# Two early units' products on GpSimd, and token, weight and key steps at later places, in a fused attention and SwiGLU kernel

## The chip, the cores and the metric

The kernel runs on one core of one Trainium2 chip. The metric is the device time of one execution in microseconds (us); the figure for a kernel is the median of its runs. The engines are named as in the profile: PE is TensorE, DVE is VectorE, ACT is ScalarE, POOL is GpSimd, SP is the queue that issues most DMAs.

## The reference

Inputs are q, k, v of 4 batches, 4 heads, 1088 positions and 32 values each, two sketches S1 and S2 of 8 x 32, and the weights of a feed-forward block with 128 inputs and 1536 hidden columns.

```python
def phi(x):
    a = einsum('rd,bhsd->bhsr', S1, x)
    b = einsum('rd,bhsd->bhsr', S2, x)
    return einsum('bhsi,bhsj->bhsij', a, b).reshape(*x.shape[:-1], 64)
q_p, k_p = phi(q), phi(k)
kv  = einsum('bhsf,bhsd->bhfd', k_p, v)
z   = sum(k_p, axis=2)
num = einsum('bhsf,bhfd->bhsd', q_p, kv)
den = einsum('bhsf,bhf->bhs', q_p, z)[..., None] + 1e-06
x   = (num / den), heads side by side: 4352 tokens x 128
g   = x @ w_gate;  silu = g / (1 + exp(-g));  val = x @ w_val
out = (silu * val) @ w_out
```

## The kernel before

**Blocks and units.** The 4352 tokens are cut into ten blocks. Blocks 0, 1, 2 are batch 0 (384, 320 and 384 tokens); blocks 3 to 9 are the other batches in pieces of 480 (the last 384). The 1536 hidden columns are cut into 12 chunks of 128. A *unit* (i, j) is block i times chunk j: two products on TensorE (gate and value), SiLU of the gate on ScalarE, and the product of both, kept as `hidden[i, j]`. A *down* step (L1068) multiplies it with chunk j of w_out and sums it over j in PSUM.

**Plain units.** `unit` (L1008 to L1033) does a unit with fp32 matmuls: L1016 for gate and value, L1020 the SiLU into `sg`, and L1031 on VectorE, `sg` times the value in PSUM, into `hbuf` (or `late`, further rooms of the same kind). With `late=True` VectorE is left out: the SiLU goes to a slot of `room`, ScalarE copies the value out of PSUM (L1028), and the pair is put on the list `lates`. `catch_up` (L1037 to L1040) takes the oldest pair from that list and multiplies it on GpSimd. Four units are late before the change: (0,0), (0,1), (0,2), (1,0).

**Split units.** From (2,6) on, units use cut operands. `start_unit` (L974) multiplies the differences xd and wd for gate and value (L980) and scales the sums in place on ScalarE (L983). `finish_unit` (L985) adds the products of the upper and lower parts (L992, L993), then SiLU (L995) and the product on VectorE (L1000). Start comes one or two units ahead of finish. Three pairs of PSUM banks go round, so a start needs the pair that an L1000 has read.

**Cutting.** `cut_weights` (L839) cuts a group c of three chunks of w_gate or w_val in four steps, one at each call: w1 on ScalarE (L843), low = w - w1 (L846), wb on ScalarE (L848), wd (L851 on VectorE or L855 on GpSimd). Names like `v0`, `g1` in the code are the steps of w_val group 0 and w_gate group 1. Groups 2 and 3 belong to chunks 6 to 11, which block 2 uses first; groups 0 and 1 to chunks 0 to 5, which block 3 uses first. Groups g0, g1 and all v are cut on GpSimd. `cut_tokens` (L857) cuts a block's tokens in two steps: for block 2 (`x`) and block 3 it is L865 on ScalarE and L873 (xd) on VectorE in the first, L868 (x0) on VectorE in the second.

**Attention of the later batches.** `attentions` (L615) is a generator; `parts_of(1)` runs its next part, and `group()` the parts that hold TensorE work. For batch 1, 2 and 3: transposes of keys (`turn_keys`, L327) and queries (L578), products of keys with the sketches (L354), key features (L377), their sums on GpSimd (L547), sums with the values (L388, L713), `fold` on VectorE (L601, L605, L608, which writes a third sketch), `spread_out` (L723), products of the queries with the three sketches (L342), `query_step` (L741 to L758, ending in phT), and `numerators` (L776 on TensorE, L793 copies into the tokens xT).

**Order.** Everything is issued by hand, in program order on each engine. Which step stands where is set by tables: `steps_at` names cutting steps by the place in the loop after which they are issued (the three loops at L1305, L1327 and L1341, and the `while todo` loop at L1350, where the key is the number of down steps left), calls of `catch_up`, and the calls of `parts_of`. An engine takes its instructions in that order; an instruction that waits keeps all behind it on its engine.

**Batch 0, third step.** Around 20 to 30 us the features of block 2's queries (L461 copies on ScalarE, L475 on VectorE), their totals (L497 on TensorE) and the division (L518 to L539) are issued among the units (1,1), (1,2) and (0,3). Weights arrive as 64-bit words and are made fp32 in steps (L263 to L286), of which L286 for chunks 3 to 5 of w_val runs on GpSimd.

Of the kernel before, what the change touches and what calls it, by code (L numbers as in the profile page):

```python
# [19 lines left out]
def kernel(  # L20
# [91 lines left out]
    def bank(tag=None):  # L112

        if tag is not None:
            i = place[tag]
        else:
            i = place[free_banks[turn[0] % len(free_banks)]]
            turn[0] += 1
        touch(i)
        return PS[:, i, :]  # L120

    def pair(keep=None):

        i = min((i for i in (0, 4, 6) if i not in held), key=lambda i: max(used[i], used[i + 1]))
        touch(i, i + 1)
        if keep is not None:
            held.add(i)
            kept[keep] = i
        return PS[:, i : i + 2, :]
# [183 lines left out]
    late = const.tile([P, NL, BW], FP32, tag="late", name="late", bufs=1)  # L313
# [153 lines left out]
    def query_features(n, pss, qbs=None, phq=None, pairs=(0, 1)):  # L467
        w = 32 * n
        if phq is None:
            phq = apool.tile([P, H, 32 * XS], FP32, tag="phq", name="phq", bufs=2)  # L470
        qbs = qbs or [query_copy(n, *ps) for ps in pss]
        for pr in pairs:
            (both, parts), qb = pss[pr], qbs[pr]
            if both is not None:
                nc.vector.tensor_tensor(  # L475
                    out=phq[:, 2 * pr : 2 * pr + 2, 0:w],
                    in0=both[:, :, 0, 0:w], in1=qb[:, :, 0:w], op=ALU.mult,
                )
            else:
                for g in range(2):  # L480
                    nc.vector.tensor_tensor(
                        out=phq[:, 2 * pr + g, 0:w],
                        in0=parts[g][:, 0, 0:w], in1=qb[:, g, 0:w], op=ALU.mult,
                    )
        return phq

    def halves(x):
        return x if isinstance(x, list) else [x[:, 0, :], x[:, 1, :]]

    def totals(n, phq, kvz, nd, which=(1, 0)):  # L490

        w = 32 * n
        for t in which:
            for h in range(H):
                for half in range(2):
                    r = slice(F * half, F * half + F)
                    nc.tensor.matmul(  # L497
                        halves(nd[t])[half][32 * h : 32 * h + 32, 0:w],
                        kvz[t][r, 32 * h : 32 * h + 32],
                        phq[r, h, 0:w],  # L500
                        start=True,
                        stop=True,
                    )
        return nd

    def side_by_side(tag):
        both = wide(tag)[:].rearrange("p g (t w) -> p g t w", t=2)
        return both[:, :, 0, :], both[:, :, 1, :]
# [291 lines left out]
    todo = []  # L800
# [56 lines left out]
    def cut_tokens(i, engine=nc.gpsimd, soon=False):  # L857

        t0, n = blocks[i]
        x = xT[:, t0 : t0 + n]  # L860
        x1, x0, xd = x_parts[i] = [
            apool.tile([P, WB], F32R, tag=tag, name=name, bufs=2)
            for tag, name in (("qb", "x1"), ("dT", "x0"), ("rd", "xd"))
        ]
        nc.scalar.activation(x1[:, 0:n], x, AF.Copy, scale=CUT)  # L865

        def low():
            engine.tensor_tensor(  # L868
                out=x0[:, 0:n], in0=x, in1=whole(x1[:, 0:n]), op=ALU.subtract
            )  # L870

        def difference():
            nc.vector.scalar_tensor_tensor(  # L873
                out=xd[:, 0:n], in0=whole(x1[:, 0:n]), scalar=WHOLE, in1=x,
                op0=ALU.mult, op1=ALU.subtract,
            )


        first, second = (difference, low) if soon else (low, difference)
        first()  # L880
        yield
        second()
# [91 lines left out]
    def start_unit(i, j):  # L974

        n = blocks[i][1]
        xd = x_parts[i][2][:, 0:n]
        ps = sums_of[i, j] = pair((i, j))[:, :, 0:n]
        for k, w in enumerate((wg, wv)):
            nc.tensor.matmul(  # L980
                ps[:, k], w_parts[id(w), j // 3][2][:, j % 3, :], xd, start=True, stop=True
            )
        nc.scalar.activation(ps, ps, AF.Copy, scale=-1.0 / WHOLE)  # L983
# [24 lines left out]
    def unit(i, j, late=False, between=(None, None), apart=False):  # L1008


        t0, n = blocks[i]
        g, u = halves(pair()) if apart else (bank(), bank())
        for o, w in ((g, wg), (u, wv)):
            if between[0] and w is wv:
                between[0]()
            nc.tensor.matmul(  # L1016
                o[:, 0:n], w[:, j, :], xT[:, t0 : t0 + n], start=True, stop=True
            )
        sg = room[:, len(lates) + caught[0], :] if late else fpool.tile([P, WB], FP32, tag="sg", name="sg", bufs=5)
        nc.scalar.activation(sg[:, 0:n], g[:, 0:n], AF.Silu)  # L1020
        slot_of[i, j] = slots.pop(0)
        hj = slot_of[i, j]
        hidden[i, j] = hj
        todo.append((i, j))
        if late:
            if between[1]:
                between[1]()
            nc.scalar.copy(hj[:, 0:n], u[:, 0:n])  # L1028
            lates.append((hj[:, 0:n], sg[:, 0:n]))
        else:  # L1030
            nc.vector.tensor_tensor(  # L1031
                out=hj[:, 0:n], in0=sg[:, 0:n], in1=u[:, 0:n], op=ALU.mult
            )  # L1033
# [3 lines left out]
    def catch_up():  # L1037
        o, sg = lates.pop(0)
        caught[0] += 1
        nc.gpsimd.tensor_tensor(out=o, in0=o, in1=sg, op=ALU.mult)  # L1040
# [89 lines left out]
    def part(name, i):  # L1130

        next(fills[name, i], None)
# [47 lines left out]
    n = steps[0][1]  # L1180
# [50 lines left out]
    def parts_of(n):  # L1231

        for _ in range(n):
            if ahead[0] not in ("pe", "end"):
                ahead[0] = next(att, "end")
# [21 lines left out]
    qbs = [query_copy(steps[2][1], *ps) for ps in pss]  # L1257
    part("wv", 2)
    part("wg", 2)
    unit(1, 1)  # L1260
    phq = query_features(steps[2][1], pss, qbs)
    part("wv", 2)
    for _ in range(3):
        catch_up()
    unit(1, 2)
    nd = totals(steps[2][1], phq, kvz, side_by_side("a"))
    divide(0, *steps[2], nd)

# [25 lines left out]
    def at(*names):  # L1294
        for name in names:
            next(cuts[name], None)

    def next_down():
        if order:
            todo.remove(order[0])  # L1300
            todo.insert(0, order.pop(0))
        down()

    steps_at = {20: ("v2",), 21: ("v3", "v2", "v3"), 22: ("g2",), 23: ("g3",)}
    for z, (i, j) in enumerate(seq):  # L1305
# [15 lines left out]

    steps_at = {
        0: ("g2", "v2", "v3"), 1: ("g2",), 2: ("g2", "g3"), 3: ("g3", "v2"), 4: ("g3", "v3"), 5: ("g2",),
        6: ("x",), 7: ("x",), 8: ("g3", "v0"), 9: ("g0",), 10: ("v0",), 11: ("g0",),
    }
    ND = 13
    for n in range(ND):  # L1327
        if n == ND - 2:
            start_unit(2, 6)
        next_down()  # L1330
        parts_of(n in (0, 1, 7, 10, 11, 12))
        at(*steps_at.get(n, ()))
        if n == 5:
            catch_up()


    steps_at = {
        6: ("v0",), 7: ("g0",), 8: ("v1",), 9: ("g1",), 10: ("v0",), 11: ("g0", "v1"),
    }
    todo.sort(key=lambda x: (order + [x]).index(x))  # L1340
    for j in range(6, NCH):  # L1341
# [4 lines left out]
        parts_of(1)  # L1346
        at(*steps_at.get(j, ()))
    x_steps = iter(())
    steps_at = {9: ("g1",), 8: ("v1",), 6: ("g1",), 4: ("v1", "g1")}
    while todo:  # L1350
        if len(todo) == 2:
            start_unit(HEAD, 0)
        next_down()
        at(*steps_at.get(len(todo), ()))
        next(x_steps, None)
        if len(todo) == 7:
            parts_of(1)
            x_steps = cut_tokens(HEAD, nc.vector, soon=True)
            next(x_steps)
        if len(todo) < 5:  # L1360
            parts_of(1)

    flat = hbuf[:].rearrange("p s w -> p (s w)")
# [73 lines left out]
```

## Time and profile before

| what | before |
|---|---|
| median of 3 runs | 281.86 us (281.56 to 281.90) |
| profiled execution | 281.39 us, of which the span of the trace is 279.7 us |
| PE busy | 269.9 us, 97% of the span |
| DVE busy | 208.6 us, 75% |
| ACT busy | 188.9 us, 68% |
| POOL busy | 102.7 us, 37% |
| granted TensorE clock | 1.00 |
| DVE busy in 60 to 70 us, 90 to 100 us | 9.90 of 10, 9.38 of 10 |
| POOL busy in 60 to 70 us, 70 to 80 us, 90 to 100 us | 8.72, 6.97, 6.45 of 10 |

The span is the stretch between the first and the last instruction of the trace; the 1.69 us around it are counted in the device time. Busy times come from the profiled execution. A line of a timeline gives the start from the span's begin, the duration, engine, source line, operation, what is written and read, the shapes, how many instructions are merged, and in brackets the idle time just before with the engine and line that ended it. A duration includes time in which an instruction was held up after its start. An fp32 matmul of the program shows as two in the trace.

### The profile page before, as it was taken

To read this page: it belongs to the slowest core of one execution; us is meant where nothing else is said; L and a number is where in the kernel's file an instruction comes from. 1 tells how busy PE (TensorE), PEld (TensorE's weight loads), DVE (VectorE), ACT (ScalarE), POOL (GpSimd) and SP (SyncE) were. 2 spreads that over 40 slices of the span, in tenths; PEclk is the share of its full clock that TensorE was granted. 3 is DMA by queue.
4 is the path that set the end of the run, shared out by engine and by line. 5 is a ranking of instruction groups with operands and counts; after the bars stand their busy time and mean duration, and the time that the engine had idled before them with its cause. 6 is when DMAs were issued, how large, how long until landed. Compare 5 with 4: busy or idle time off the path is not lost.

```text
span 279.7 us, 5723 instructions
## 1 busy us (share of the span) xinstructions
PE 269.9 (97%) x2181; PEld 199.7 (71%) x2181; DVE 208.6 (75%) x355; ACT 188.9 (68%) x335; POOL 102.7 (37%) x112
## 2 busy tenths in 40 slices
PE   7898999999999889999999999999999999999995
PEld 7554466666785577777667768767887888788994
DVE  3996988879896962787736658867986995988431
ACT  3466566362693557676658898859879888886860
POOL 3312531249852650080014452534335462632000
PEclk9999999999999999999999999999999999999999
DMA  6572287131331042100200010000100200010011
GB/s 191 166 227 60 56 237 228 40 123 56 66 87 23 2 110 60 38 1 0 35 13 6 1 28 10 0 2 8 29 0 2 35 0 1 12 25 0 8 30 28
DMA packets 26139, 14.30 MB, mean 51 GB/s; under 512 B 19840, under 2 KB 24192, under 8 KB 26112
## 3 DMA queue, kind: packets, MB, share of 16 engines
q1 hardware_dynamic: 25456, 13.84, 19.3%
q8 instruction: 17, 0.28, 0.4%
q10 hardware_dynamic: 656, 0.10, 0.2%
q14 instruction: 10, 0.08, 0.1%
HBM read 11.41 MB, written 2.23 MB: 49 GB/s over the span
## 4 chain that ended last, share of the span: by engine, by line
PE 80%; DVE 12%; ACT 2%; issue 2%; DMA 1%; POOL 0%; SPq 0%; DVEq 0%; ACTq 0%
PE PS L1068 16%; PE PS L992 13%; PE PS L980 13%; PE PS L993 13%; PE PS L1016 10%; PE PS L1060 2%; PE PS L1063 2%; PE PS L1062 2%; PE PS L776 2%; PE PS L342 2%; DVE phk L377 2%; DMA kld<-in_k_dram 1%; PE PS L354 1%; PE PS L388 1%; DVE phT L758 1%
## 5 line engine op out<-in xcount | busy, mean ns | idle before, releaser
L983 ACT ACTIVATE PS<-PS 128x960 f32<-128x960 f32 (+1 forms) x90 | 83.3, 926 | 34.0 <-PE PS L980 33.1
L1000 DVE SCALAR_TENSOR_TENSOR hbuf<-PS,sg 128x480 f32<-128x480 f32 (+1 forms) x87 | 55.2, 634 | 42.9 <-ACT sg L995 40.3
L995 ACT ACTIVATE sg<-PS 128x480 f32<-128x480 f32 (+1 forms) x90 | 49.7, 552 | 2.6 <-ACT sg L995 1.3
L1068 PE MATMUL PS<-hbuf,wo 128*128 128x480 f32 (+3 forms) x118 | 45.8, 488 | 0.0
L980 PE MATMUL PS<-xd,graw 128*128 128x480 f32 (+1 forms) x69 | 38.2, 554 | 0.0
L980 PE MATMUL PS<-xd,wd 128*128 128x480 f32 (+1 forms) x90 | 33.5, 372 | 1.7 <-DVE hbuf L1000 1.7
L993 PE MATMUL PS<-x,wb 128*128 128x480 f32 (+1 forms) x90 | 33.4, 372 | 0.0
L992 PE MATMUL PS<-x,w 128*128 128x480 f32 (+1 forms) x90 | 33.4, 371 | 0.0
L1068 PEld LDWEIGHTS PS<-hbuf,wo 128*128 128x128 f32 x118 | 22.0, 189 | 5.6 <-issue 0.4
L980 PEld LDWEIGHTS PS<-xd,wd 128*128 128x128 f32 x90 | 17.0, 189 | 12.2 <-issue 5.8
L993 PE MATMUL PS<-x,graw 128*128 128x480 f32 (+1 forms) x69 | 25.5, 370 | 0.0
L1016 PE MATMUL PS<-xT,wv 128*128 128x384 f32 (+1 forms) x60 | 23.2, 468 | 0.6 <-POOL wv L286 0.3
L1016 PE MATMUL PS<-xT,wg 128*128 128x384 f32 (+1 forms) x60 | 23.5, 474 | 0.1
L1020 ACT ACTIVATE sg<-PS 128x384 f32<-128x384 f32 (+1 forms) x26 | 11.9, 466 | 15.7 <-PE PS L1016 14.8
L868 POOL TENSOR_TENSOR x<-xT,x 128x480 fp32r<-128x480 f32 (+1 forms) x6 | 7.2, 1192 | 39.5 <-ACT x L865 39.5
L980 PEld LDWEIGHTS PS<-xd,graw 128*128 128x128 f32 x69 | 13.0, 188 | 7.7 <-ACT PS L983 4.1
L992 PEld LDWEIGHTS PS<-x,w 128*128 128x128 f32 x90 | 16.9, 187 | 2.2
L993 PEld LDWEIGHTS PS<-x,wb 128*128 128x128 f32 x90 | 16.9, 188 | 2.1
L992 PE MATMUL PS<-x,graw 128*128 128x480 f32 (+1 forms) x48 | 18.4, 384 | 0.0
L1068 PE MATMUL PS<-hbuf,scaled 128*128 128x480 f32 x36 | 17.4, 564 | 0.0
L1016 PEld LDWEIGHTS PS<-xT,wv 128*128 128x128 f32 x60 | 11.1, 190 | 7.8 <-DVE hbuf L1031 1.0
L960 POOL TENSOR_TENSOR hlate<-hbuf,hlate 128x480 fp32r<-128x480 f32 x10 | 12.9, 1289 | 9.8 <-ACT hlate L959 7.7
(196 smaller groups left out, 541.1 us busy)
## 6 DMA issues: line engine op xcount, KB each, us to landing
kld<-in_k_dram SPq DMA_DIRECT2D x4, 544.0 KB, 4.0
vld<-in_v_dram SPq DMA_DIRECT2D x12, 144.0 KB, 4.0
qld<-in_q_dram SPq DMA_DIRECT2D x3, 544.0 KB, 3.4
raw<-in_moe_w_out_dram SPq DMA_DIRECT2D x4, 384.0 KB, 5.6
raw<-in_moe_w_gate_dram SPq DMA_DIRECT2D x3, 384.0 KB, 3.4
raw<-in_moe_w_val_dram SPq DMA_DIRECT2D x3, 384.0 KB, 3.1
out_dram<-o SPq DMA_DIRECT2D x16, 60.0 KB, 2.0
vld<-in_v_dram SPq DMA_DIRECT2D x4, 112.0 KB, 3.2
```

Source lines behind the costliest of these rows:

```text
L342: nc.tensor.matmul(ps[32 * a : 32 * a + 32, 96 * (c - c0) : 96 * (c - c0) + 96], qT[:, 4 * c + a, :], s123[:, a : a + H, :, :].rearrange(" ...
L868: engine.tensor_tensor(out=x0[:, 0:n], in0=x, in1=whole(x1[:, 0:n]), op=ALU.subtract)
L960: add_to(before, y + 2, lambda: nc.gpsimd.tensor_tensor(out=h0, in0=h, in1=whole(h1), op=ALU.subtract))
L980: nc.tensor.matmul(ps[:, k], w_parts[id(w), j // 3][2][:, j % 3, :], xd, start=True, stop=True)
L983: nc.scalar.activation(ps, ps, AF.Copy, scale=-1.0 / WHOLE)
L992: nc.tensor.matmul(ps[:, k], w1, x1, start=False, stop=False, skip_group_check=True)
L993: nc.tensor.matmul(ps[:, k], wb, x0, start=False, stop=True, skip_group_check=True)
L995: nc.scalar.activation(sg, ps[:, 0], AF.Silu, scale=WHOLE)
L1000: nc.vector.scalar_tensor_tensor(out=hj[:, 0:n], in0=ps[:, 1], scalar=WHOLE, in1=sg, op0=ALU.mult, op1=ALU.mult)
L1016: nc.tensor.matmul(o[:, 0:n], w[:, j, :], xT[:, t0 : t0 + n], start=True, stop=True)
L1020: nc.scalar.activation(sg[:, 0:n], g[:, 0:n], AF.Silu)
L1068: nc.tensor.matmul(acc[i][:, 0:n], w, hidden[i, j][:, 0:n], **sides)
```

## The change

Units (1,1) and (1,2) become late: L1031 on VectorE is replaced by the SiLU into `room`, the copy L1028 on ScalarE, and the product on GpSimd, and two more calls of `catch_up` are issued after the one that was there. The two steps of `x`, the token cut of block 2, are issued one place later, the first behind the part of `attentions` that holds the fold. The last two steps of `v0` and `g0`, and all steps of `v1` and `g1`, are issued later. In the last loop `parts_of` is called for 2, 3 and 4 remaining down steps and no longer for 1 and 0, so that the following parts (the keys' transposes of batch 3, then the queries' of batch 2) are issued from the next loop, which finishes a unit of block 3 before each.

```diff
-    unit(1, 1)
+    unit(1, 1, late=True)
     phq = query_features(steps[2][1], pss, qbs)
     part("wv", 2)
     for _ in range(3):
         catch_up()
-    unit(1, 2)
+    unit(1, 2, late=True)
...
     steps_at = {
         0: ("g2", "v2", "v3"), 1: ("g2",), 2: ("g2", "g3"), 3: ("g3", "v2"), 4: ("g3", "v3"), 5: ("g2",),
-        6: ("x",), 7: ("x",), 8: ("g3", "v0"), 9: ("g0",), 10: ("v0",), 11: ("g0",),
+        7: ("x",), 8: ("x", "g3", "v0"), 9: ("g0",), 10: ("v0",), 11: ("g0",),
     }
...
         at(*steps_at.get(n, ()))
-        if n == 5:
+        if n in (5, 6, 7):
             catch_up()
...
     steps_at = {
-        6: ("v0",), 7: ("g0",), 8: ("v1",), 9: ("g1",), 10: ("v0",), 11: ("g0", "v1"),
+        9: ("v0",), 10: ("g0", "v0"), 11: ("g0",),
     }
...
-    steps_at = {9: ("g1",), 8: ("v1",), 6: ("g1",), 4: ("v1", "g1")}
+    steps_at = {8: ("v1", "g1", "v1", "g1"), 6: ("v1", "g1"), 1: ("v1", "g1")}
...
-        if len(todo) < 5:
+        if len(todo) in (2, 3, 4):
             parts_of(1)
```

## Prediction

> **What bounds the kernel now.** I read the page first (busy times, then the chain that ended last), then what TensorE waited for, then the timelines of TensorE, VectorE, ScalarE and GpSimd around each of those waits. All times are us of the profiled execution: span 279.7, device time 281.39.
>
> ```profile
> PE 80%; DVE 12%; ACT 2%; issue 2%; DMA 1%; POOL 0%; SPq 0%; DVEq 0%; ACTq 0%
> ```
>
> ```profile
> PE PS L980 <- DVE hbuf L1000: 1.7, 1, 1.7
> PE PS L497 <- DVE phq L475: 1.0, 1, 1.0
> ...
> PE PS L342 <- DVE s L608: 0.3, 1, 0.3
> PE PS L1016 <- POOL wv L286: 0.3, 1, 0.3
> ...
> PE PS L776 <- DVE phT L758: 0.2, 1, 0.2
> ```
>
> TensorE has 97% busy and 80% of the chain. So only what shortens its few waits counts. The columns of the second view are waiter, releaser, us in total, times, longest. Listed are the five waits that the change can touch; they lie at 26.1 (L497), 28.5 (L1016), 72.7 (L342), 87.5 (L776) and 98.8 (L980). From 100 to 270 us it is busy 10.00 of every 10 us but once (9.92 from 180), so what is won before 100 is kept.
>
> Idle is measured to the modelled end of the last matmul, which lies later than the next one could start. I therefore count starts:
>
> ```profile
> 24.44 0.70 PE L1016 MATMUL PS<-xT,wv 128*128 128x320 f32 x2
> 26.11 1.23 PE L497 MATMUL PS<-phq,kvz 64*32 64x192 f32 x32 [0.96 <-DVE phq L475]
> 27.27 0.91 PE L1016 MATMUL PS<-xT,wg 128*128 128x384 f32 x2
> 28.49 0.91 PE L1016 MATMUL PS<-xT,wv 128*128 128x384 f32 x2 [0.31 <-POOL wv L286]
> ```
>
> Columns: start, duration, instruction. A 320-wide pair takes 0.54 from start to start elsewhere (23.90 to 24.44), a 384-wide one 0.645 (29.24 to 29.88). So L497 could start at about 25.08 (0.1 for the change of shape), 1.03 earlier, and the last line at 27.27 + 0.645, 0.57 earlier. The same count gives 0.5 at 72.7, 0.35 at 87.5, 1.85 at 98.8.
>
> Why is L475 late? VectorE and ScalarE there:
>
> ```profile
> 25.01 0.49 DVE L1031 TENSOR_TENSOR hbuf<-sg,PS 128x320 f32<-128x320 f32 x1 [2.30 <-ACT sg L1020]
> 25.41 1.01 DVE L475 TENSOR_TENSOR phq<-PS,qb 128x384 f32<-128x384 f32 x2
> ```
>
> VectorE stands still for 2.30 until the SiLU of unit (1,1) is there, at the head of its queue, while the data of L475 behind it (qb, L461, 22.85 to 23.72) is ready.
>
> The last wait, 98.8, is VectorE's queue again (first fence), with GpSimd beside it (second fence):
>
> ```profile
> 91.19 1.45 DVE L868 TENSOR_TENSOR x<-xT,x 128x480 fp32r<-128x480 f32 x1
> ...
> 94.64 1.77 DVE L377 TENSOR_TENSOR phk<-kab 128x512 f32<-128x512 f32 x1
> 96.34 0.83 DVE L327 STREAM_TRANSPOSE kT<-kld 128x640 f32<-128x640 f32 x1
> 97.10 0.53 DVE L1110 STREAM_TRANSPOSE o<-PS 128x384 f32<-128x384 f32 x1
> 97.56 0.66 DVE L327 STREAM_TRANSPOSE kT<-kld 128x512 f32<-128x512 f32 x1
> 98.16 0.61 DVE L1000 SCALAR_TENSOR_TENSOR hbuf<-PS,sg 128x480 f32<-128x480 f32 x1
> ```
>
> ```profile
> 91.08 1.05 POOL L855 TENSOR_TENSOR graw<-gphq,graw 128x384 fp32r<-128x384 f32 x1 [4.09 <-ACT graw L848]
> 94.28 1.58 POOL L547 TENSOR_TENSOR zs<-phk 128x512 f32<-128x512 f32 x1 [2.15 <-PE PS L1068]
> ```
>
> L1000 of (3,0), whose SiLU was done at 96.2, comes after two key transposes and an output transpose. And two VectorE operations are stretched exactly while GpSimd runs: L377 of 512 takes 0.67 alone and 1.77 beside L547.
>
> [...] (L868 1.45 beside L855; L377 1.77 beside L547; L377 with one input in PSUM 0.67 to 0.94 also beside GpSimd). The trace adds that they take turns: L547 asked at 94.28 and ran before the L377 that was queued for 94.64. [...] here 0.87 (L1040, 320 wide) against 0.47 (L1031). [...]
>
> **The change, part by part.** The order of instructions on TensorE and of the DMAs on SP is the same in both kernels, so only waits can change.
>
> (1) Units (1,1), (1,2) late. Off VectorE: two L1031, before L475 and before L518. Onto ScalarE: two L1028 of 0.44, behind the SiLUs: 24.64 + 4 steps of about 0.35 = 26.05. TensorE wants the banks that they free from 26.3 on; nothing else waits there (next ScalarE work is a SiLU at 27). Then VectorE: L475 at 23.35 and 23.85, done 24.3; L271 and L277 (their ScalarE inputs are done at 24.2 and 24.6), done 25.3; L286 on GpSimd 1.00, done 26.35. TensorE: L497 at 25.08, the next unit at 26.25, its second half wanted at 26.9, after L286. **Gain 1.03 + 0.57 = 1.6.** Weights, transposes and DMAs up to 60 us are issued after VectorE steps that wait for TensorE (L1031 <- PE L1016), so they move along; the w_out loads land before 47 and are read at 52. The two L1040 of 0.87 on GpSimd come after 72; TensorE reads their results at 80 and 81.7, slack over 4.
>
> From here I use the old clock; the 1.6 applies to all.
>
> (2) Token differences behind the fold. L873 (1.28, of which some 0.65 is a wait for GpSimd's L855) leaves the place before L601. L713 ends at 70.57, so the fold can begin at 70.6, and L608 be ready at 71.15. [...] L608 ends at 72.35 instead of 72.65. **Gain 0.3 at L342.** The ends: 0.5 if L608 gets in first, 0 if not earlier at all. Now L873 is what can be late: TensorE's L980 wants xd at 74.0. Taking turns with L1040 (0.87 each): L873 73.2 to 73.8, L868 74.65 to 75.2, L741 76.05 to 76.45 (75.9 before). Slack 0.2, just hidden; if one more turn is lost it costs 0.7.
>
> (3) Splits of groups 0 and 1 later. Of the four ScalarE steps L848/L843 of 0.52, each goes behind three more units; they lie in gaps of ScalarE (68% busy). GpSimd's two L846 are pushed to 76.5 to 78.9 by the L1040s, so the L377 at 78 is blocked as before (78.9 to 79.8; before 79.9). L855 of group 0 moves from 78.1/79.7 to about 82.5 and 83.8. Then VectorE: L1000 (2,8) 81.65, L377 82.5, L1000, L1110, L758 84.4, L1000 84.85, L377 85.7, L1000 86.15, L758 87.05 against 87.49. **Cumulative gain at L776 0.4** (range -0.3 to 0.7).
>
> Group 1's L848s now stand behind L865 on ScalarE (90.5, 90.9), so both L855 of group 1 fall on 91 to 93.6 where only one did. TensorE wants them at 96.75, slack 3. But L868 is then blocked by the first as before and the L377 of 768 by the second: **minus 1.0**, from the 1.05 of L855.
>
> (4) Keys' transposes behind the first later unit. They leave the way of L1000 (3,0): 0.7 + 0.6, **gain 1.3 to 1.4**. Later L1000s have 0.55 + 0.7 per unit of 1.3 on TensorE: just covered. L354 reads kT 3.8 after the wait's end; ready 1.8 after. Behind them the L578s and the load of batch 3's queries on SP (issued at 100.7) follow about 1 later in relation; the next L578 reads that load at 112.1, and such a load lands in 3.4, so some 7 are spare. With (3), net at 98.8: 1.4 - 1.0 = 0.4.
>
> Sum: 1.6 + 0.4 + 0.4 = **2.4**: 281.39 - 2.4 = 279.0 for the profiled execution. It stands 0.47 under the median of 281.86, so **279.5** for the median.
>
> **Rivals.**
> R2, [...] (VectorE's L377 follows L868 at once, L855 waits): 1.0 more, 278.5. For: in the span 85.2, L377 kept 0.93 while L855 needed 1.54. Against: the turn at 94.28.
> R3, only the first part pays: the later waits are filled anew, by xd at L980 (0.7) or by L1000 coming too late for a pair of banks (slack 0.15 to 0.2), which eats the 0.8: 281.86 - 1.6 = 280.3. For: thin slacks. Against: L342 and L1000 do get shorter queues.
> R4, slower: GpSimd's longer queue at 72 (three L1040, two L846: 3 x 0.87 + 2 x 1.0 = 4.6) [...] L873, now behind the fold, waits for all of it. xd at 77.3 instead of 74.0: TensorE stands 3 at L980, L776 starts 2.7 late. 281.86 - 1.6 + 2.7 - 0.4 = 282.6. It decides from a block of about 3.2 at L873 (2.4 of gains plus the slack of 0.2 and the noise). For: the queue is full there. Against: before, L873, L868 and L608 each lost at most 0.65 to a queue just as full.
> That the change does nothing is excluded by the order of instructions on VectorE.
>
> **Chances.** Forecast 0.48, R2 0.22, R3 0.21 (a fifth of it within 0.2% of no change), R4 0.09. About 0.2%, 0.6 us, is what can be told from no change. Faster 0.87, same 0.04, slower 0.09. The range of 278.1 to 281.0 takes in R2 with 0.4 more (L608 first, L758 early), and R3 with 0.7 more; beyond lies R4 and a rest.
>
> **What would show it.** Right: L497 at about 25.1 and no wait at L1016 behind it; L342 without or with less wait; L475 right after L461; both L855 of group 1 between L865 and L547, one L377 of 768 near 1.8; L1000 (3,0) right after L1110, and a wait at L980 near 1.3. Wrong: a new wait of TensorE at L980 <- DVE xd L873, or at L1068 <- POOL L1040; a wait at L980 for L855; any new wait after 100.

## The result, and the profile after

The median after the change is **279.12 us** (278.80 to 279.51, 4 runs) against 281.71 (281.47 to 281.90, 4 runs) beside it: ratio 0.9909, 95% interval 0.9892 to 0.9926. That is 2.6 us less, with 279.5 forecast and 278.1 to 281.0 as the range. The profiled execution after took 279.51, with a span of 277.8. Three runs of the experiments below took 451, 544 and 1525 us, where no other took more than 284, and are left out of all figures.

That span is only 1.9 shorter, because the starts of the program differ. The first L354, which waits for the first keys from memory, begins at 6.0 in the profile before and at 6.6 after, and the value product of (1,2) at 24.44 and 25.10. The change is not the reason: the units-alone run below has that product at 24.52. I therefore compare starts within a section, never clock times across kernels.

The chain that ended last, after:

```profile
PE 91%; DVE 5%; DMA 2%; issue 1%; ACT 1%; SPq 0%
```

TensorE's waits after (waiter, releaser, us in total, times, longest):

```profile
PE PS L980 <- DVE hbuf L1000: 1.2, 1, 1.2
...
PE PS L776 <- DVE phT L758: 0.3, 1, 0.3
PE PS L1016 <- DVE wv L286: 0.3, 1, 0.3
```

VectorE had 12% of the chain and has 5%. Of the five waits that were followed, L497 <- L475, L342 <- L608 and L1016 <- GpSimd's L286 are gone; the L1016 that is listed now is another one, which waited for VectorE in the kernel before, too. L776 went from 0.2 to 0.3, and L980 from 1.7 to 1.2.

TensorE after, around the first two:

```profile
25.10 0.70 PE L1016 MATMUL PS<-xT,wv 128*128 128x320 f32 x2
25.73 0.88 PE L497 MATMUL PS<-phq,kvz 64*32 64x192 f32 x32
26.54 0.91 PE L1016 MATMUL PS<-xT,wg 128*128 128x384 f32 x2
27.29 0.81 PE L1016 MATMUL PS<-xT,wv 128*128 128x384 f32 x2
```

L497 follows (1,2) by 0.63 instead of 1.67. It also takes less itself: 0.81 to the next start instead of 1.16. That row merges 32 matmuls, and in the kernel before a second wait is hidden in it. It shows in TensorE's weight loads (PEld), before:

```profile
26.07 0.18 PEld L497 LDWEIGHTS PS<-phq,kvz 64*32 64x32 f32 x8 [1.44 <-ACT sg L1020]
26.48 0.48 PEld L497 LDWEIGHTS PS<-phq,kvz 64*32 64x32 f32 x24 [0.22 <-DVE phq L475]
```

The first eight belong to the half of phq that the first L475 writes. The rest wait for the second L475, which ends at 26.42. After the change both L475 are done at 25.05, and the 32 loads stand in one row of 0.51.

The value product of (0,3) follows by 0.75 instead of 1.22. There is a small price further on: the gate product of (0,5) starts at 29.23 and its value product at 30.05, 0.82 later where 0.645 is usual. Its weight load waits for VectorE's L1031 of (0,3), which frees the banks and ends at 30.00:

```profile
30.05 0.30 PEld L1016 LDWEIGHTS PS<-xT,wv 128*128 128x128 f32 x2 [0.63 <-DVE hbuf L1031]
```

The other sections, from start to start, are below ("L388" is the first L388 of batch 2).

| section, us | before | after |
|---|---|---|
| value product of (1,2) to L388 | 43.46 | 41.71 |
| L388 to L342 | 4.80 | 4.41 |
| L388 to L776 | 19.63 | 19.33 |
| L776 to the L980 that waits | 11.29 | 10.79 |

The gains are 1.75, 0.39, then -0.09 between L342 and L776, and 0.50: together 2.55, against 2.59 between the medians. There is nothing left to explain after 100 us.

At L342, VectorE after:

```profile
69.54 0.22 DVE L601 TENSOR_TENSOR fold<-PS,sq 128x64 f32<-128x64 f32 x1 [0.19 <-PE PS L713]
...
70.10 0.23 DVE L608 TENSOR_TENSOR s<-w,own 128x64 f32<-128x64 f32 x1
...
70.41 1.20 DVE L873 SCALAR_TENSOR_TENSOR xd<-x,xT 128x384 fp32r<-128x384 f32 x1
```

and GpSimd beside it:

```profile
68.90 1.32 POOL L855 TENSOR_TENSOR wd<-w,wb 128x384 fp32r<-128x384 f32 x1
...
70.18 1.01 POOL L855 TENSOR_TENSOR wd<-w,wb 128x384 fp32r<-128x384 f32 x1
```

L608 takes 0.23: the second L855 did not hold it up. L873 and the L868 behind it take turns with GpSimd as forecast: they take 1.20 and 1.22, of which some 0.6 each is a wait (in the run with the cuts in the gap, where GpSimd stands still beside them, even the wider ones of block 3 take 0.66 and 0.65), and the first L1040 beside them takes 1.19, where the third has 0.85. TensorE nowhere waits for xd.

At L980, VectorE after:

```profile
89.80 1.45 DVE L868 TENSOR_TENSOR x<-xT,x 128x480 fp32r<-128x480 f32 x1
91.17 1.75 DVE L377 TENSOR_TENSOR phk<-kab 128x768 f32<-128x768 f32 x1
...
95.76 0.57 DVE L1110 STREAM_TRANSPOSE o<-PS 128x384 f32<-128x384 f32 x1
96.26 0.61 DVE L1000 SCALAR_TENSOR_TENSOR hbuf<-PS,sg 128x480 f32<-128x480 f32 x1
96.80 0.82 DVE L327 STREAM_TRANSPOSE kT<-kld 128x640 f32<-128x640 f32 x1
```

and GpSimd:

```profile
89.69 1.05 POOL L855 TENSOR_TENSOR wd<-w,wb 128x384 fp32r<-128x384 f32 x1 [3.14 <-ACT wb L848]
90.70 1.41 POOL L855 TENSOR_TENSOR graw<-gphq,graw 128x384 fp32r<-128x384 f32 x1
```

L1000 now stands right behind the output transpose L1110, and the L327 follows it. In exchange both L855 of group 1 fall here, and each stretches the VectorE instruction beside it: L868 takes 1.45, as in the kernel before, and the first L377 1.75, where the kernel before has 0.94.

### The profile page after: what moved, and what is told of

It is laid out like the page before. It is cut to its first block, busy times and chain, and to the rows that moved or that the text cites. A ratio compares the mean times of both kernels' runs of the same rounds, so it can differ in the third digit from the quotient of the medians.

```text
span 277.8 us, 5723 instructions
## 1 busy us (share of the span) xinstructions
PE 270.1 (97%) x2181; PEld 200.5 (72%) x2181; DVE 208.2 (75%) x353; ACT 189.8 (68%) x337; POOL 104.8 (38%) x114
## 4 chain that ended last, share of the span: by engine, by line
PE 91%; DVE 5%; DMA 2%; issue 1%; ACT 1%; SPq 0%
PE PS L1068 21%; PE PS L980 14%; PE PS L992 14%; PE PS L993 13%; PE PS L1016 12%; PE PS L1060 2%; PE PS L1063 2%; PE PS L1062 2%; PE PS L354 2%; PE PS L776 2%; PE PS L342 2%; DMA kld<-in_k_dram 2%; PE PS L388 2%; PE PS L1096 1%; PE PS L497 1%
## 5 line engine op out<-in xcount | busy, mean ns | idle before, releaser
L1000 DVE SCALAR_TENSOR_TENSOR hbuf<-PS,sg 128x480 f32<-128x480 f32 (+1 forms) x87 | 55.2, 635 | 42.2 <-ACT sg L995 39.7
L980 PE MATMUL PS<-xd,graw 128*128 128x480 f32 (+1 forms) x69 | 38.2, 554 | 0.0
L980 PE MATMUL PS<-xd,wd 128*128 128x480 f32 (+1 forms) x90 | 33.5, 373 | 1.2 <-DVE hbuf L1000 1.2
L980 PEld LDWEIGHTS PS<-xd,wd 128*128 128x128 f32 x90 | 17.0, 189 | 11.7 <-issue 6.0
L1016 PE MATMUL PS<-xT,wg 128*128 128x384 f32 (+1 forms) x60 | 23.5, 474 | 0.1
L1016 PE MATMUL PS<-xT,wv 128*128 128x384 f32 (+1 forms) x60 | 23.2, 468 | 0.3 <-DVE wv L286 0.3
L868 POOL TENSOR_TENSOR x<-xT,x 128x480 fp32r<-128x480 f32 (+1 forms) x6 | 7.2, 1192 | 38.2 <-ACT x L865 38.2
L1020 ACT ACTIVATE sg<-PS 128x384 f32<-128x384 f32 (+1 forms) x24 | 11.1, 467 | 13.2 <-PE PS L1016 12.4
L980 PEld LDWEIGHTS PS<-xd,graw 128*128 128x128 f32 x69 | 13.0, 189 | 7.7 <-ACT PS L983 4.0
L1016 PEld LDWEIGHTS PS<-xT,wv 128*128 128x128 f32 x60 | 11.2, 190 | 7.3 <-DVE hbuf L1031 0.8
```

What stands on the lines that cost most here:

```text
L868: engine.tensor_tensor(out=x0[:, 0:n], in0=x, in1=whole(x1[:, 0:n]), op=ALU.subtract)
L980: nc.tensor.matmul(ps[:, k], w_parts[id(w), j // 3][2][:, j % 3, :], xd, start=True, stop=True)
L1000: nc.vector.scalar_tensor_tensor(out=hj[:, 0:n], in0=ps[:, 1], scalar=WHOLE, in1=sg, op0=ALU.mult, op1=ALU.mult)
L1016: nc.tensor.matmul(o[:, 0:n], w[:, j, :], xT[:, t0 : t0 + n], start=True, stop=True)
```

## The experiments

The theory is that of the forecast: each of the four moves changes one queue, and the waits add up. The rivals are R2 (the second L855 costs VectorE nothing at 91 to 94), R3 (only the first part pays), R4 (GpSimd's queue makes xd late) and, for part (1), that the work taken from VectorE matters and not its place. All runs stand beside the kernel before, whose median was 281.75 in the first session (units alone, without units, splits back, cuts in the gap) and 281.65 in the second (the other four). The ratios of the second session lie 0.1 to 0.3% under those of the medians, since 8 of the 26 runs of the kernel before took 283.0 to 283.8 there; what a part is worth is therefore read from the sections.

**Each half alone.** The late units alone, on the kernel before:

```diff
-    unit(1, 1)
+    unit(1, 1, late=True)
-    unit(1, 2)
+    unit(1, 2, late=True)
-        if n == 5:
+        if n in (5, 6, 7):
             catch_up()
```

> The kernel before with part (1) alone: units (1,1) and (1,2) late, the two more GpSimd products behind 72 us. Theory (the head of VectorE's queue): the first part is worth about 1.7 us by itself; the two L1040 lengthen GpSimd's queue before L846, which may hold up VectorE around 73 to 78 and cost up to 0.3 at L776. 280.0 to 280.4 against 281.7, L497 follows unit (1,2) within 0.65 instead of 1.67. Rival (the parts only pay together, since a later wait on VectorE takes the gain back): under 0.8 faster, with a longer wait at L776 or L980.

Measured: 280.10 (279.89 to 281.25, 6 runs), ratio 0.9943 (0.9924 to 0.9962). The first section is 41.71, as after; the others are those of before (4.80, 19.63, 11.29).

The kernel after without these three edits:

> The changed kernel with part (1) undone: fold, splits and transposes as changed, units (1,1), (1,2) on VectorE as before. Theory: the parts add up, so what is left of the gain is 2.6 - 1.7 = 0.9, of which 0.4 at L342, -0.1 at L776 and 0.5 at L980; 280.8. The wait of 1.0 at L497 is back. Rival (parts not additive): anything outside 0.5 to 1.3 faster than before.

Measured: 281.13 (280.76 to 282.39, 12 runs), ratio 0.9973 (0.9955 to 0.9992). The sections are 43.46 for the first and those of after for the rest (4.41, 19.33, 10.79). So the halves do not touch each other: 1.75 by the sections (1.65 by the medians) for the units, 0.80 (0.6) for the rest. R3 is refuted: the later waits are not filled anew. The second half is small, but its interval excludes 1.

**The place or the work.** On the kernel before, both products stay on VectorE, but are issued together behind the integer steps L271 and L277, so behind L475:

```diff
-    unit(1, 1)
+    unit(1, 1, back=(back := []))
     phq = query_features(steps[2][1], pss, qbs)
...
-    unit(1, 2)
+    unit(1, 2, back=back), [f() for f in back]
```

In `unit`, the argument `back` makes a list of the L1031 instead of issuing it.

> The kernel before with one edit: the two L1031 of units (1,1) and (1,2) stay on VectorE but are issued together behind L277, just before L518. No work is taken off VectorE. Theory (what counts is what stands at the head of the queue): TensorE's waits at L497 and L1016 go as in the change, 1.5 to 1.8 faster than before, about 280.1. Rival (VectorE is relieved of work): the two times 0.4 put L518 to L539 later, and less than half of it, under 0.8, is won.

Measured: 279.80 (279.61 to 280.06, 6 runs), ratio 0.9921 (0.9896 to 0.9947). Its VectorE:

```profile
23.42 1.02 DVE L475 TENSOR_TENSOR phq<-PS,qb 128x384 f32<-128x384 f32 x2 [0.67 <-ACT qb L461]
...
25.29 0.88 DVE L1031 TENSOR_TENSOR hbuf<-sg,PS 128x320 f32<-128x320 f32 x2
```

L475 comes straight behind its copies, as after. The section to L388 is 41.71, the same 1.75 without GpSimd and without the two copies on ScalarE. It is the place in the queue that paid. The 0.88 of work came later, where VectorE had time.

**The token cut back ahead of the fold**, on the kernel after:

```diff
-        7: ("x",), 8: ("x", "g3", "v0"), 9: ("g0",), 10: ("v0",), 11: ("g0",),
+        6: ("x",), 7: ("x",), 8: ("g3", "v0"), 9: ("g0",), 10: ("v0",), 11: ("g0",),
```

> The changed kernel with part (2) undone: L865 and L873 of block 2 before the fold, L868 behind it. Theory: L608 ends later again and L342 waits, 0.4 by starts. Whether it reaches the end depends on the wait at L776: the query chain on VectorE is paced by TensorE's units, so it moves along, and the kernel is 0.2 to 0.4 slower than the changed one, about 279.4. Rival: L776 waits for VectorE anyway, and the 0.3 there takes it up; within 0.15 of the changed kernel.

Measured: 279.60 (279.17 to 279.81, 6 runs), ratio 0.9914 (0.9886 to 0.9942). TensorE has the wait again:

```profile
70.84 1.69 PE L342 MATMUL PS<-s,qT 128*32 128x96 f32 x72 [0.32 <-DVE s L608]
```

L388 to L342 is 4.79 (after: 4.41), and L388 to L776 is 19.72 (19.33). What is lost at L342 reaches L776 whole. The median is 0.5 above the 279.12 of the kernel after, which ran in another session; that is about what medians can tell, so what this part is worth rests on the sections.

**The keys' transposes back ahead**, on the kernel after:

```diff
-        if len(todo) in (2, 3, 4):
+        if len(todo) < 5:
             parts_of(1)
```

> The changed kernel with part (4) undone: both key transposes stand before the first L1000 of block 3 again. Theory: that L1000 comes 0.7 + 0.6 later, the wait at L980 grows from 1.19 to about 2.5; 1.3 slower than the changed kernel, about 280.4. Rival (what is late at L980 is set by something else, and the transposes fit beside it): within 0.3 of the changed kernel.

TensorE's wait at L980:

```profile
97.58 0.48 PE L980 MATMUL PS<-xd,wd 128*128 128x480 f32 x1 [2.49 <-DVE hbuf L1000]
```

L776 to L980 is 12.10 instead of 10.79: the part is worth 1.31. The times fall into two groups. Eight runs took 280.20 to 280.56 (middle 280.44, as expected); in thirteen the mean granted clock was 0.992 to 0.994 instead of 0.998 to 1.000, and they took 281.7 to 283.4 (middle 281.94). So the median is 281.81 and the ratio 0.9981 (0.9961 to 1.0000). The last section comes back to that clock.

**The splits back**, on the kernel after, with the tables of v0, g0, v1 and g1 as before:

```diff
-        9: ("v0",), 10: ("g0", "v0"), 11: ("g0",),
+        6: ("v0",), 7: ("g0",), 8: ("v1",), 9: ("g1",), 10: ("v0",), 11: ("g0", "v1"),
...
-    steps_at = {8: ("v1", "g1", "v1", "g1"), 6: ("v1", "g1"), 1: ("v1", "g1")}
+    steps_at = {9: ("g1",), 8: ("v1",), 6: ("g1",), 4: ("v1", "g1")}
```

> The changed kernel with part (3) undone: the steps of v0, g0, v1, g1 at their old places, all else as changed. Theory [...]: only one L855 falls on 89 to 91 us again, so L377 of 768 takes 0.94 instead of 1.75 and the wait at L980 shrinks from 1.19 to about 0.4; at L776 the L377s are held up elsewhere and the sum is about the same. 0.8 faster than the changed kernel, about 278.3: the later splits were a loss in the change. Rival (the later splits free ScalarE and VectorE and are part of the gain): 0.3 to 1.0 slower than the changed kernel, with a longer wait at L776.

Measured: 278.24 (278.06 to 279.64, 6 runs), ratio 0.9877 (0.9857 to 0.9898), 0.9 less than the kernel after. Its VectorE ahead of L980 (the row holds four L377):

```profile
90.92 3.85 DVE L377 TENSOR_TENSOR phk<-kab 128x768 f32<-128x768 f32 x4
```

The same row in the kernel after:

```profile
91.17 4.66 DVE L377 TENSOR_TENSOR phk<-kab 128x768 f32<-128x768 f32 x4
```

That is 0.81 more. TensorE's wait at L980 is 0.36, and L776 to L980 is 9.98, also 0.81 less than 10.79. R2 is refuted: the second L855 does cost here. So part (3) of the change loses, and the rest gains more than the whole.

**The splits where VectorE stands still.** VectorE waits 1.7 for L776 in the profiles before and after, from about 86 on in that of after. The last two steps of v1 and g1 (L848, L855) stand at 6 and 1 remaining down steps. Issued at 7, ahead of the copies L793, they should put both L855 there; on the kernel after:

```diff
-    steps_at = {8: ("v1", "g1", "v1", "g1"), 6: ("v1", "g1"), 1: ("v1", "g1")}
+    steps_at = {8: ("v1", "g1", "v1", "g1"), 7: ("v1", "g1", "v1", "g1")}
```

> The changed kernel with the last two steps of v1 and g1 (L848, L855) issued before the copies L793, so that both L855 run at 86.6 to 88.6 us, where VectorE stands still behind L776. Theory [...]: L868 takes 0.6 instead of 1.45 and L377 of 768 takes 0.94 instead of 1.75, 1.6 together, and the wait at L980 (1.19, 1.35 by starts) is gone; 1.2 to 1.35 faster than the changed kernel, about 277.8. Rival (VectorE's queue is long enough by itself, or L868 and L377 are slow for another reason): within 0.3 of the changed kernel. Rival (L848 in front of L793 on ScalarE delays the tokens): slower by up to 0.7.

Measured: 277.98 (277.60 to 278.24, 5 runs), ratio 0.9861 (0.9842 to 0.9880). Its GpSimd, then its VectorE:

```profile
86.35 1.00 POOL L855 TENSOR_TENSOR wd<-w,wb 128x384 fp32r<-128x384 f32 x1
87.31 0.99 POOL L855 TENSOR_TENSOR graw<-gphq,graw 128x384 fp32r<-128x384 f32 x1
```

```profile
89.64 0.65 DVE L868 TENSOR_TENSOR x<-xT,x 128x480 fp32r<-128x480 f32 x1
90.20 3.85 DVE L377 TENSOR_TENSOR phk<-kab 128x768 f32<-128x768 f32 x4
```

Both L855 are over by 88.30. Until then VectorE waits for L776 and copies out of PSUM (L793, 87.64 to 88.33; its 0.69 is that of the kernel after, where no GpSimd work is beside it). L868 is at 0.65 instead of 1.45 and the four L377 at 3.85 instead of 4.66. TensorE no longer waits at L980.

**And group 0 early**, since the L377 of 768 just ahead of L776 was stretched in the kernel after. To the edit above this adds:

```diff
-        9: ("v0",), 10: ("g0", "v0"), 11: ("g0",),
+        6: ("v0",), 7: ("g0",), 10: ("v0",), 11: ("g0",),
```

> As the run with the cuts in the gap, and the last two steps of v0 and g0 at their old, earlier places. Theory [...]: both L855 of group 0 fall on 76.5 to 79.2 and cost the first L377 there 0.3, which waits for TensorE's units anyway; the third L377 of the query features (1.64 in the changed kernel) is free and takes 0.94, so the wait of 0.3 at L776 goes too. 1.5 to 1.7 faster than the changed kernel, about 277.5. Rival: the chain to L776 is paced by the units[...] and the time is that of the run with the cuts in the gap.

Measured: **277.28** (277.23 to 277.48, 5 runs), ratio 0.9833 (0.9806 to 0.9861), the best of all and 1.8 under the kernel after. L388 to L776 is 18.94 instead of 19.33. VectorE in the kernel after, then here:

```profile
77.17 0.94 DVE L377 TENSOR_TENSOR phq<-qab 128x768 f32<-128x768 f32 x1
...
83.09 1.64 DVE L377 TENSOR_TENSOR phq<-qab 128x768 f32<-128x768 f32 x1
```

```profile
76.62 1.29 DVE L377 TENSOR_TENSOR phq<-qab 128x768 f32<-128x768 f32 x1
...
82.69 0.93 DVE L377 TENSOR_TENSOR phq<-qab 128x768 f32<-128x768 f32 x1
```

The L377 of query features that is stretched is now an early one, and the last one, on which L776 hangs, is not. TensorE waits neither at L776 nor at L980.

## Why the prediction was right

**Part (1), 1.6 forecast, 1.75 measured.** The mechanism holds: L497, and with it all behind, came earlier by what VectorE's queue gave free, and the place-only run shows that it is the wait of 2.30 for the SiLU at the head of VectorE's queue. L497 came 1.04 earlier (1.03 forecast). Three terms differ. L497's own length was taken as fixed, but fell by 0.35, since the forecast saw only the first of its two waits for L475. The value product of (0,3) won 0.47 (0.57 forecast): its turn came so early that its weights, done by L286 on GpSimd at 27.08, were just late, and its weight load began at 27.13. And 0.18 went to the banks freed late by L1031 of (0,3), which the forecast had not counted; about 0.1 of it was left at L388.

**Part (2), 0.3 forecast, 0.39 measured.** The step that failed, an estimate, put L608 behind GpSimd's second L855 (71.1 to 72.1), so that it ends at 72.35. L608 took 0.23, where the kernel before has 0.46 (72.19 to 72.65, with two L855 on record to 72.56). By the timeline it came just where one L855 gave way to the next: the first, which had begun beside VectorE's L851, is on record to 70.22, L608 from 70.10 to 70.33, and the second L855 from 70.18 with its usual 1.01, so neither lost. That is the better end of the forecast's own range ("0.5 if L608 gets in first"). The forecast had put L608 ready at 71.15 and the second L855 from 71.1, so which would be first was luck. The xd that now comes later was done at 71.61 and wanted at 72.84, so R4 is refuted.

**Parts (2) and (3) at L776, 0.4 forecast, 0.30 measured.** The 0.4 is counted from L388 and holds the 0.3 at L342. Part (3) by itself was thus put at +0.1 and is -0.09; the splits-back run, whose L388 to L776 is 19.24, gives the same 0.09. The total is near the forecast by luck, since two errors cancel. The step said that the L377 at 78 is blocked "as before" by the L846s and the later ones are free. It was the other way round. By the timeline, with L608 ahead of the second L855, L873 and what follows on both engines came a turn earlier than forecast, and the L846s were done at 76.46. (The forecast's clock is 1.09 ahead of this one, by the first L388: 77.55 there, where it had 78.9.) So the L377 at 77.17 took 0.94, and VectorE came to the last L377 about 0.6 earlier than forecast, at 83.09 (84.18 on the forecast's clock, where it has the L1000 ahead of it done at 84.85). There it met GpSimd's L855 of g0 (first fence) and took 1.64, where the kernel before has 0.93 (second fence):

```profile
82.92 1.00 POOL L855 TENSOR_TENSOR gphq<-gphq 128x384 fp32r<-128x384 f32 x1 [0.57 <-ACT gphq L848]
```

```profile
85.19 0.93 DVE L377 TENSOR_TENSOR phq<-qab 128x768 f32<-128x768 f32 x1
```

That is 0.71 at the one place without slack. I had laid the two queues side by side, but with the turns in the wrong order, and did not ask which L377 has slack. The group-0-early run takes this stretch away: the last L377 is at 0.93 and the section 0.39 shorter.

**Parts (3) and (4) at L980, +0.4 forecast, 0.50 measured.** Part (4) was put at 1.3 to 1.4 and is 1.31. The second L855 was put at -1.0, an estimate from the 1.05 of an L855, and is -0.81, the stretch of L377 from 0.94 to 1.75. It is on record from 90.70, beside L868 (to 91.25), and L377 from 91.17, so it may have been partly done when L377 came up.

The forecast's three terms, 1.6, 0.4 and 0.4, measured 1.75, 0.30 and 0.50: 2.55 for 2.4. The mechanism held: the time came from what stood at the head of VectorE's queue when TensorE waited for it. The closeness of the sum is partly luck, for the 0.35 that was not counted in (1) met some 0.2 of losses, and the errors at L776 cancelled. The likeliest case held. R2, R3 and R4 are refuted by the splits-back run, by the two halves, and by the absence of a wait for xd, in this order.

## What to carry to other kernels

Look for the instruction that waits at the head of a queue with ready work behind it: moving it past that work gave 1.75 us here, and moving it to another engine gave no more. Before you put GpSimd work at a new place, lay it beside VectorE's queue and ask which of VectorE's instructions there has slack: the same two L855 stretch VectorE by 1.6 (0.80 in L868, 0.81 in L377) at one place, and by nothing where VectorE waits for TensorE (L793 beside them keeps its 0.69). Undo a change part by part even when it wins: this one held a part that loses 0.9. And where a row of the timeline merges many instructions, look for a second wait inside it: the 0.35 of L497 showed only in its weight loads.

## What the runs showed of the hardware that was not expected

**Half the clock behind a wait, in some runs.** The units-alone kernel's profiled execution took 281.25, above its other runs. TensorE in stretches of that profile (stretch, length, busy and instructions, granted clock, DMA share, GB/s):

```profile
97.40:97.60 0.20, 0.20 (x2) 0.50 0.82 134
...
98.00:100.00 2.00, 2.00 (x7) 0.50 0.27 42
...
100.60:100.80 0.20, 0.20 (x2) 0.57 1.31 326
100.80:101.00 0.20, 0.20 (x3) 1.00 0.65 239
```

Right behind the wait of 1.68 at L980 the clock is 0.50 for 3.4 us (97.4 to 100.8), and matmuls of 480 columns start 0.40 apart, where the kernel before has 0.22 (99.15 to 99.37):

```profile
97.15 0.61 PE L980 MATMUL PS<-xd,wd 128*128 128x480 f32 x1 [1.68 <-DVE hbuf L1000]
97.55 0.60 PE L992 MATMUL PS<-x,gphq 128*128 128x480 f32 x1
```

From there to the next L388 it takes 4.15 (97.15 to 101.30), where the kernel before takes 2.60 (98.82 to 101.42).

Only this profile shows the dip itself. Its mean clock is 0.992; in the other runs a mean clock of 0.992 to 0.994 is taken for its sign. In the two sessions, such runs were 13 of 21 with a wait of 2.49 (the transposes-back kernel), 7 of 55 with one of about 1.7 (before, units alone, place only), and none of 34 with 1.2 or less (the other five kernels). In the transposes-back kernel they are 1.5 us longer than the rest. So a shorter wait at L980 goes with fewer such runs. That the wait is the cause is only argued, from this order and from the place of the dip; a wait of a set length was not tried. Nor does it explain every long run: eight runs with a mean clock of 0.998 or more (five of the kernel before, two without units, one with the splits back) are 1.2 to 1.5 above their kernels' medians, and no profile of one was kept.
